# Splitting a table tile in two, holding back later transfers, and a third matmul in place of a vector sum in the first 14 of 256 steps

## The chip, the cores and the metric

One core of a Trainium2 chip runs the whole kernel. The metric is the device time of one execution in microseconds (us), and smaller is better. Each kernel was executed several times, with runs of the kernel before on the same chip beside it. All times compared below are of the fast state. One run of the kernel before (1415.36 us) was disturbed; it stands in the quoted range and medians of the first rounds, not in any ratio.

## The reference, cut to what matters

```python
# x: 8 x 3136 x 256, w_in: 256 x 1024, conv_w: 3 x 1024, w_out: 1024 x 256, float32 and float64
X = np.fft.fft(x, axis=1)
X = np.fft.fft(X, axis=2).real.astype(np.float32)
h = np.maximum(X @ w_in, 0.0)
conv_out = sum(conv_w[k] * shifted(h, k - 1) for k in range(3))   # along the sequence, zeros at the ends
gate = 1.0 / (1.0 + np.exp(-conv_out))
out = (h * gate @ w_out).astype(np.float32)
```

The kernel writes the transform along the sequence as products with tables of cosines and sines. For each batch it makes two arrays, `PT` and `QT`, over half of the sequence positions. With the transform along the features folded into the first weight matrix (`G`), `A` comes from `PT` and `B` from `QT`. The hidden row is relu(A + B) on the front half of the sequence and relu(A - B), mirrored, on the back half.

## The kernel before

The tables lie in one tile with six slots. Slots 0 and 1 serve the even frequencies, 2 and 3 the odd ones, and 4 and 5 are copies of 3 and 2 with changed signs.

```python
    tab = const.tile([P, 6, HQ, HE], F32, name="tab")
    ...
    def load_tables(par):
        st = slice(2 * par, 2 * par + 2)
        to = tab[:, st].rearrange("p s q i -> p s (q i)")
        for i in range(2):
            nc.sync.dma_start(out=to[i:NP:2], in_=dft_seq[0:NP // 2, st, HQ * i:HQ * (i + 1)] ...)

    def mend_tables(par, half):                      # runs on ScalarE
        st = slice(2 * par, 2 * par + 2)
        row = tab[96:NP, st, HQ - 1]
        act(row, row, AF.Copy, scale=half[96:NP])                              # L216
        if par:
            for i in range(2):
                for to, of, s in ((4, 3, -1.0), (5, 2, 1.0)):
                    act(tab[0:KR, to, :, i:HO:2], tab[0:KR, of, :, i:HO:2], AF.Copy,   # L220
                        scale=-s if i else s)
    ...
    for par in (1, 0):
        mend_tables(par, half)
    ...
    for i, u in enumerate(us[j] for j in (0, 1, 4, 2, 3, 5, 6, 7, 8)):   # the transform of batch 0
        u.matmuls(0, 1)
        u.copy()                                     # ScalarE
        if i == 2:
            flip()
        u.fin()                                      # VectorE
        if i < 2:
            w_in[0].narrow(i, slice(0, H))           # VectorE: float64 weights to float32
        ...
```

`us` lists the units of the transform: 0 and 1 use the odd tables, 4 (the last feature, with matmuls of one column, `ea`) and 2, 3 the even ones, 5 and 6 the odd ones again, 7 and 8 the even ones.

Then 256 steps follow, each for one batch, one of four chunks of the sequence and one of eight blocks of 128 hidden features. Before a step's products, ScalarE writes the last feature's part of A into `pa` (the "seed", L499), from a row `er` that was broadcast by DMA and a column `ge` of the folded weights. `pa` and `pb`, which PE writes, lie in PSUM; the other tiles lie in SBUF:

```python
    def products(s):                                 # PE
        mm(pb[s][:, 0:n], G[0:P - 1, 1, fs], PQ[b][1][0:P - 1, ch.k0:ch.k1], True, True)     # B
        mm(pa[s][:, 0:n], G[:, 0, fs], PQ[b][0][:, ch.k0:ch.k1], False, True)                # A, onto a seed
    def copies(s):                                   # ScalarE: +B and -B into SBUF
        for i, cols in enumerate((ch.fcols, ch.cols)):
            act(nb[s][:, i, cols], p[:, cols], AF.Copy, scale=-1.0 if i else 1.0)            # L514
    def combine(s):                                  # VectorE: two sums with relu
        for i, (to, cols) in enumerate(((h[:, ch.front], ch.fcols), (h[:, ch.back][:, ::-1], ch.cols))):
            nc.vector._custom_dve(TENSOR_ADD_SAT, out=to, in0=a[:, cols], in1=c[:, i, cols], s0=BIG, s1=0.0)  # L525
    ...
    def gate(s):
        v, p, r = shares(s)                          # two halves of the row
        gt(g[:, p], g[:, p], h[:, p], op=ALU.mult)   # GpSimd, L557
        vt(g[:, v], g[:, v], h[:, v], op=ALU.mult)   # VectorE, L558
```

Between `combine` and `gate` lie a first tap on ScalarE, two taps on VectorE and the sigmoid on ScalarE. After `gate` the second product runs on PE (`mm2`). In the first steps VectorE narrows the rest of the weights too (L402 to L409) and folds the input of batch 1 (L151 to L179). In program order `gate` of a step is followed on VectorE by `combine` of a later step and then by that side work.

## Time and profile before

| kernel before | |
|---|---|
| time, median of 3 runs | 1278.77 us (1276.97 to 1415.36) |
| PE begins the transform | 46.08 us |
| first sum of the main loop (L525) | 70.98 us |
| step 14's gate product on VectorE (L558) starts | 173.19 us |

In the views PE is TensorE's matmuls and PEld its weight loads, DVE is VectorE, ACT ScalarE, POOL GpSimd; L525 is line 525 of the kernel's file. The granted clock is the share of full speed that TensorE had. First, two lines of the start: ScalarE's copy of unit 0, which follows PE's start at 46.08, and the one-column products of the even unit 4 (start us, us, what, and in brackets the idle time before and what ended it):

```profile
48.44 0.32 ACT L282 COPY as<-po 128x196 f32<-128x196 f32 x1 [1.45 <-PE po L90]
...
52.96 0.89 PE L90 MATMUL po<-tab,ea 99*1 99x197 f32 x16
```

### The profile page before, as it was taken

To read this page: it belongs to the slowest core of one execution; us is meant where nothing else is said; L and a number is where in the kernel's file an instruction comes from. 1 tells how busy PE (TensorE), PEld (TensorE's weight loads), DVE (VectorE), ACT (ScalarE), POOL (GpSimd) and SP (SyncE) were. 2 spreads that over 40 slices of the span, in tenths; PEclk is the share of its full clock that TensorE was granted. 3 is DMA by queue.
4 is the path that set the end of the run, shared out by engine and by line. 5 is a ranking of instruction groups with operands and counts; after the bars stand their busy time and mean duration, and the time that the engine had idled before them with its cause. 6 is when DMAs were issued, how large, how long until landed. Compare 5 with 4: busy or idle time off the path is not lost.

```text
span 1277.4 us, 15522 instructions
## 1 busy us (share of the span) xinstructions
PE 1178.4 (92%) x4850; PEld 887.1 (69%) x4850; DVE 1148.4 (90%) x1753; ACT 885.1 (69%) x1835; POOL 397.6 (31%) x500
## 2 busy tenths in 40 slices
PE   0567799999999999999999999999999999999997
PEld 0345567767777777777677776777777777777776
DVE  4579998999999989899989989999999878899996
ACT  0244676777767777777777777776777778788884
POOL 3311643424342315242423414242222212222222
PEclk9988999999999999999999999999999999999999
DMA  8420321202031103020111202120010001011000
GB/s 212 121 63 1 119 69 31 83 28 76 27 94 32 56 25 95 25 83 25 39 57 51 61 25 88 32 67 16 25 44 32 30 26 38 23 32 34 26 25 30
DMA packets 47179, 66.07 MB, mean 52 GB/s; under 512 B 5684, under 2 KB 35276, under 8 KB 47096
## 3 DMA queue, kind: packets, MB, share of 16 engines
q1 hardware_dynamic: 41668, 51.93, 13.5%
q0 software_dynamic: 5120, 12.85, 3.6%
q8 instruction: 39, 0.64, 0.2%
q14 instruction: 44, 0.36, 0.1%
q10 hardware_dynamic: 308, 0.29, 0.1%
HBM read 39.26 MB, written 25.74 MB: 51 GB/s over the span
## 4 chain that ended last, share of the span: by engine, by line
PE 64%; DVE 21%; issue 5%; DMA 4%; ACT 4%; POOL 1%; SPq 0%; DVEq 0%; ACTq 0%; POOLq 0%
PE po L90 40%; PE pb L90 9%; PE pa L90 9%; PE pd L90 6%; DVE g L537 6%; DVE h L525 4%; DMA tab<-dft_seq_dram 3%; DVE g L558 3%; ACT nb L514 2%; DVE xh L151 1%; DVE xh L162 1%; DVE w L178 1%; ACT g L550 1%; DVE w L179 1%; DVE xh L167 0%
## 5 line engine op out<-in xcount | busy, mean ns | idle before, releaser
L90 PE MATMUL po<-wout,g 128*128 128x256 f32 x3072 | 716.3, 383 | 37.5 <-DVE g L558 34.0
L90 PEld LDWEIGHTS po<-wout,g 128*128 128x128 f32 x3072 | 579.7, 191 | 200.7 <-DVE g L558 78.4
L537 DVE SCALAR_TENSOR_TENSOR g<-h,cw,g 128x770 f32<-128x770 f32 (+1 forms) x512 | 555.2, 1084 | 10.6 <-ACT g L531 1.5
L557 POOL TENSOR_TENSOR g<-g,h 128x385 f32<-128x385 f32 (+1 forms) x256 | 240.7, 941 | 762.6 <-ACT g L550 544.2
L550 ACT ACTIVATE g<-g 128x385 f32<-128x385 f32 (+2 forms) x512 | 244.4, 528 | 223.2 <-DVE g L537 223.0
L514 ACT ACTIVATE nb<-pb 128x386 f32<-128x386 f32 (+3 forms) x512 | 225.6, 494 | 83.5 <-PE pb L90 82.6
L525 DVE CUSTOM_DVE_ANT_0 h<-pa,nb 128x386 f32<-128x386 f32 (+3 forms) x512 | 264.8, 558 | 0.9 <-PE pa L90 0.9
L531 ACT ACTIVATE g<-h,cw 128x770 f32<-128x770 f32 (+1 forms) x256 | 243.6, 951 | 0.2 <-DVE h L525 0.2
L90 PE MATMUL pb<-qt,G 127*128 127x387 f32 (+2 forms) x512 | 214.3, 499 | 2.6 <-ACT nb L514 2.4
L90 PE MATMUL pa<-pt,G 128*128 128x387 f32 (+2 forms) x512 | 212.6, 496 | 0.4 <-DVE pt L267 0.4
L499 ACT ACTIVATE pa<-eb,ge 128x387 f32<-128x387 f32 (+2 forms) x256 | 154.0, 602 | 3.1 <-DVE h L525 3.1
L558 DVE TENSOR_TENSOR g<-g,h 128x385 f32<-128x385 f32 (+1 forms) x256 | 151.3, 591 | 1.2 <-ACT g L550 1.2
L90 PEld LDWEIGHTS pa<-pt,G 128*128 128x128 f32 x512 | 96.9, 189 | 74.3 <-issue 18.9
L90 PE MATMUL pd<-tab,w 99*128 99x196 f32 (+2 forms) x448 | 117.4, 374 | 0.0
L90 PEld LDWEIGHTS pb<-qt,G 127*128 127x128 f32 x512 | 93.9, 190 | 25.8 <-ACT nb L514 4.7
L126 POOL DMA_INDIRECT xh<-in_x_dram,idx x64 | 95.9, 1498 | 18.1 <-issue 12.3
L90 PEld LDWEIGHTS pd<-tab,w 99*128 99x128 f32 (+1 forms) x448 | 82.9, 190 | 12.8
L577 ACT COPY os<-po 128x256 f32<-128x256 f32 x196 | 58.1, 397 | 10.6 <-PE po L90 6.2
L151 DVE TENSOR_TENSOR xh<-xh 98x1020 f32<-98x1020 f32 (+1 forms) x32 | 44.4, 1391 | 12.6 <-DMA xh<-in_x_dram,idx 10.3
L90 PE MATMUL po<-tab,w 98*128 98x196 f32 (+4 forms) x64 | 18.0, 442 | 38.3 <-POOL w L182 25.9
L90 PEld LDWEIGHTS po<-tab,w 98*128 98x128 f32 (+1 forms) x64 | 13.3, 224 | 42.0 <-POOL w L182 26.0
L162 DVE TENSOR_TENSOR xh<-xh 98x1024 f32<-98x1024 f32 (+1 forms) x32 | 40.1, 1252 | 0.1
(93 smaller groups left out, 365.2 us busy)
## 6 DMA issues: line engine op xcount, KB each, us to landing
out_dram<-os SPq DMA_DIRECT2D x192, 128.0 KB
xh<-in_x_dram SPq DMA_DIRECT2D x16, 784.0 KB
eb<-ed SPq DMA_DIRECT2D x16, 193.5 KB
tab<-dft_seq_dram SPq DMA_DIRECT2D x4, 601.8 KB
raw<-in_moe_w_in_dram SPq DMA_DIRECT2D x2, 1024.0 KB
raw<-in_moe_w_out_dram SPq DMA_DIRECT2D x1, 2048.0 KB
eb<-ed SPq DMA_DIRECT2D x8, 209.0 KB
eb<-ed SPq DMA_DIRECT2D x8, 193.0 KB
```

The costliest lines, as they stand in the source:

```text
L90: nc.tensor.matmul(o, l, r, start=start, stop=stop, skip_group_check=True)
L126: nc.gpsimd.indirect_dma_start(out=xh[b, h][0:NP, 7 - m].rearrange("p q d -> p (q d)"), out_offset=None, in_=bass.AP(tensor=x.tensor, offs ...
L151: vt(a[:, :, :, 1:D], a[:, :, :, 1:D], r[:, :, :, D - 1:0:-1], op=ALU.add)
L499: act(pa[s][:, 0:n], eb[b, c], AF.Copy, scale=ge[:, f:f + 1])
L514: act(nb[s][:, i, cols], p[:, cols], AF.Copy, scale=-1.0 if i else 1.0)
L525: nc.vector._custom_dve(TENSOR_ADD_SAT, out=to, in0=a[:, cols], in1=c[:, i, cols], s0=BIG, s1=0.0)
L531: act(gs[s], hs[s][:, 0:n], AF.Copy, scale=cw[:, 0, s[2]:s[2] + 1])
L537: stt(out=g, in0=h[:, k:k + n], scalar=cw[:, k, f:f + 1], in1=g, op0=ALU.mult, op1=ALU.add)
L550: act(gs[s][:, c], gs[s][:, c], AF.Sigmoid)
L557: gt(g[:, p], g[:, p], h[:, p], op=ALU.mult)
L558: vt(g[:, v], g[:, v], h[:, v], op=ALU.mult)
L577: nc.scalar.copy(out=osb[:, j % 2], in_=pt[:, j % 2])
```

## The change

There are three intents. Each parity of tables gets a tile of its own, so that work on the odd tables need not wait for the even ones. Memsets on tiles that are about to be loaded ("holds") make later transfers wait for GpSimd's gathers of the input (in the trace after, the odd tables are issued at 9.82 us, behind a memset at 9.62; before, at 1.68); the small row of the input's second half is also issued ahead of the tables. And in the first 14 steps, where VectorE is full (busy 85.77 of 88.70 us from 71.0 to 159.7 us before), PE adds B onto A with a third product, so that ScalarE can write relu(A + B) straight from PSUM; this takes one of the two sums from VectorE. The back half still needs a sum, (A + B) - 2B.

```diff
+TRIPLE = 14
+    def hold(t):
+        nc.gpsimd.memset(t[0:1, 0, 0, 0:1], 0.0)
...
-    tab = const.tile([P, 6, HQ, HE], F32, name="tab")
+    tabs = [const.tile([P, n, HQ, HE], F32, name="tab%d" % n) for n in (2, 4)]
...
-    for f in ops[0:1] + ops[2:]:
-        f()
+    plain, zero, *mirrored = load_ops(0, 1, nc.sync, held=True)
+    plain()
+    zero()
+    for f in mirrored[0:2]:
+        f()
+    hold(tabs[1])
+    for f in mirrored[2:4]:
+        f()
     load_tables(1)
-    load_row0()
-    ops[1]()
     for i in range(2):
+        if w_in[i].raw is not None and i == 0:
+            hold(w_in[i].raw)
         w_in[i].load(nc.sync)
...
+    def triple(s):
+        return s[0] == 0 and s[1] * NF + s[2] < TRIPLE
...
-        mm(pa[s][:, 0:n], G[:, 0, fs], PQ[b][0][:, ch.k0:ch.k1], False, True)
+        mm(pa[s][:, 0:n], G[:, 0, fs], PQ[b][0][:, ch.k0:ch.k1], False, not triple(s))
+        if triple(s):
+            mm(pa[s][:, 0:n], G[0:P - 1, 1, fs], PQ[b][1][0:P - 1, ch.k0:ch.k1], False, True)
...
+        if triple(s):
+            act(nb[s][:, 1, ch.cols], p[:, ch.cols], AF.Copy, scale=-2.0)
+            row_of(s)
+            act(hs[s][:, ch.front], pa[s][:, ch.fcols], AF.Relu)
+        else:
+            for i, cols in enumerate((ch.fcols, ch.cols)):
+                act(nb[s][:, i, cols], p[:, cols], AF.Copy, scale=-1.0 if i else 1.0)
...
+            if i or not triple(s):
+                nc.vector._custom_dve(TENSOR_ADD_SAT, out=to, in0=a[:, cols], in1=c[:, i, cols],
+                                      s0=BIG, s1=0.0)
```

Line numbers shift: L216 and L220 become L223 and L227; the sums L525 become L556; GpSimd's and VectorE's gate products L557 and L558 become L588 and L589; the narrowing L402 and L403 become L409 and L410; the fold L151 becomes L158; PE's helper L90 becomes L91.

More of the change, by code (lines that the diff above doesn't have):

```diff
@@ L105, with load_ops @@
     nc.gpsimd.memset(sg[:, 1], 1.0)
-    def load_ops(b, h, eng):
+    def hold(t):
+        nc.gpsimd.memset(t[0:1, 0, 0, 0:1], 0.0)
+    def load_ops(b, h, eng, held=False):
         def plain():
@@ L112, in plain @@
             xh[b, h] = t
+            if held:
+                hold(t)
             eng.dma_start(out=t[0:NP, 0:4], in_=bass.AP(
@@ L190, in fold_ops, with table @@
         return half(0) + half(1)
-    tab = const.tile([P, 6, HQ, HE], F32, name="tab")
+    tabs = [const.tile([P, n, HQ, HE], F32, name="tab%d" % n) for n in (2, 4)]
     PQ, eb, er = {}, {}, {}
     ed = edp.tile([B, NK], F32, name="ed")
+    def table(k, st, q, cols):
+        return tabs[st // 2][0:k, st, q, cols] if st < 2 else tabs[1][0:k, st - 2, q, cols]
     def load_tables(par):
         st = slice(2 * par, 2 * par + 2)
-        to = tab[:, st].rearrange("p s q i -> p s (q i)")
+        to = tabs[par][:, 0:2].rearrange("p s q i -> p s (q i)")
         for i in range(2):
@@ L203, in load_tables @@
                               .rearrange("p s q i -> p s (q i)"))
-    def load_row0():
         n = HQ * HE
-        nc.sync.dma_start(out=tab[NP:KR, 0:4].rearrange("p s q i -> p s (q i)"), in_=bass.AP(
-            tensor=dft_seq.tensor, offset=dft_seq.offset + (NP * 4 * NQ - HQ + 2) * HE,
-            ap=[[n, 1], [NQ * HE, 4], [1, n]]))
+        nc.sync.dma_start(out=to[NP:KR], in_=bass.AP(
+            tensor=dft_seq.tensor, offset=dft_seq.offset + ((NP * 4 + 2 * par) * NQ - HQ + 2) * HE,
+            ap=[[n, 1], [NQ * HE, 2], [1, n]]))
     def mend_tables(par, half):
-        st = slice(2 * par, 2 * par + 2)
-        row = tab[96:NP, st, HQ - 1]
+        row = tabs[par][96:NP, 0:2, HQ - 1]
         act(row, row, AF.Copy, scale=half[96:NP])
@@ L218, in mend_tables @@
             for i in range(2):
-                for to, of, s in ((4, 3, -1.0), (5, 2, 1.0)):
-                    act(tab[0:KR, to, :, i:HO:2], tab[0:KR, of, :, i:HO:2], AF.Copy,
+                for to, of, s in ((2, 1, -1.0), (3, 0, 1.0)):
+                    act(tabs[1][0:KR, to, :, i:HO:2], tabs[1][0:KR, of, :, i:HO:2], AF.Copy,
                         scale=-s if i else s)
@@ L244, in f @@
             k = KR if q == HQ - 1 else NP
-            mm(p[o], w(k, q), tab[0:k, st, q, cols], start, stop)
+            mm(p[o], w(k, q), table(k, st, q, cols), start, stop)
         return f
@@ L447 @@
     nc.scalar.dma_start(out=dm, in_=dft_dim[:, :, 0:2])
-    for f in load_ops(0, 0, nc.sync):
-        f()
-    ops = load_ops(0, 1, nc.sync)
-    for f in ops[0:1] + ops[2:]:
+    ops = load_ops(0, 0, nc.sync)
+    for f in ops:
+        f()
+    plain, zero, *mirrored = load_ops(0, 1, nc.sync, held=True)
[5 more added lines that the diff above has]
+    for f in mirrored[2:4]:
         f()
     load_tables(1)
-    load_row0()
-    ops[1]()
     for i in range(2):
+        if w_in[i].raw is not None and i == 0:
+            hold(w_in[i].raw)
         w_in[i].load(nc.sync)
@@ L499, in seed, with row_of @@
         act(pa[s][:, 0:n], eb[b, c], AF.Copy, scale=ge[:, f:f + 1])
+    def triple(s):
+        return s[0] == 0 and s[1] * NF + s[2] < TRIPLE
+    def row_of(s):
+        hs[s] = hp.tile([P, HW], F32, name="h", tag="h")
+        w = chunks[s[1]].w
+        if chunks[s[1]].zeros:
+            nc.gpsimd.memset(hs[s][:, 0:w:w - 1], 0.0)
     def products(s):
@@ L512, in copies @@
         nb[s] = nbp.tile([P, 2, HN], F32, name="nb", tag="nb")
-        for i, cols in enumerate((ch.fcols, ch.cols)):
-            act(nb[s][:, i, cols], p[:, cols], AF.Copy, scale=-1.0 if i else 1.0)
+        if triple(s):
[5 more added lines that the diff above has]
+                act(nb[s][:, i, cols], p[:, cols], AF.Copy, scale=-1.0 if i else 1.0)
     def combine(s):
@@ L519, in combine @@
         a, c = pa.pop(s), nb.pop(s)
-        h = hp.tile([P, HW], F32, name="h", tag="h")
-        hs[s] = h
-        if ch.zeros:
-            nc.gpsimd.memset(h[:, 0:ch.w:ch.w - 1], 0.0)
+        if not triple(s):
+            row_of(s)
+        h = hs[s]
         for i, (to, cols) in enumerate(((h[:, ch.front], ch.fcols), (h[:, ch.back][:, ::-1], ch.cols))):
-            nc.vector._custom_dve(TENSOR_ADD_SAT, out=to, in0=a[:, cols], in1=c[:, i, cols],
-                                  s0=BIG, s1=0.0)
+            if i or not triple(s):
+                nc.vector._custom_dve(TENSOR_ADD_SAT, out=to, in0=a[:, cols], in1=c[:, i, cols],
+                                      s0=BIG, s1=0.0)
     def first_tap(s):
```

## The prediction

> **What bounds the kernel now.** I read the page first (busy shares, the 40 slices), then busy time by stretch, then the chain in order of time, then the waits of the first 70 us.
>
> ```profile
> span 1277.4 us, 15522 instructions
> PE 1178.4 (92%) x4850; PEld 887.1 (69%) x4850; DVE 1148.4 (90%) x1753; ACT 885.1 (69%) x1835; POOL 397.6 (31%) x500
> PE   0567799999999999999999999999999999999997
> DVE  4579998999999989899989989999999878899996
> DMA  8420321202031103020111202120010001011000
> ```
>
> TensorE is full from the seventh slice on; the 99 us that it lacks (1277.4 less 1178.4) lie mostly in the first six slices of 32 us, where VectorE or the transfers are full instead. By stretch:
>
> ```profile
> 0.00:33.00 33.00, 0.91 (x3) 0.85 (x4) 16.05 (x25) 2.41 (x3) 13.02 (x26) 1.00 0.83 213
> 33.00:46.00 13.00, 0.67 (x2) 0.15 (x1) 3.19 (x5) 3.21 (x4) 2.71 (x3) 1.00 0.85 204
> 46.00:69.00 23.00, 22.92 (x104) 16.79 (x104) 13.24 (x28) 6.12 (x16) 7.30 (x11) 1.00 0.31 96
> 106.40:113.60 7.20, 5.84 (x16) 4.13 (x16) 6.96 (x14) 3.04 (x8) 0.91 (x2) 0.76 0.00 1
> 145.00:149.65 4.65, 4.16 (x16) 2.96 (x16) 4.61 (x9) 3.04 (x8) 0.93 (x2) 1.00 0.46 142
> ```
>
> Columns after the length: busy us of PE, PE's weight loads, DVE, ACT, POOL, then granted clock, share of the DMA engines, GB/s. There are three stages: to 46 us almost no matmul runs, the DMA engines are 83 to 85% busy; from 46 to 69 us PE is full with the first transform; from 69 to about 165 us (the last two rows are one step each, of the 256 of the main loop) DVE is busy 97 to 99% while PE has room. After that PE leads. A microsecond taken from any of the first three stages should arrive at the end whole, as nothing later waits for the clock on the wall.
>
> The chain and the waits of the start:
>
> ```profile
> 1.68 17.59 DMA tab<-dft_seq_dram
> 20.65 21.98 DMA tab<-dft_seq_dram
> 42.79 3.24 ACT tab L220 x4
> 46.08 14.73 PE po L90 x62
> ```
> ```profile
> ACT tab L220 <- DMA tab<-dft_seq_dram: 15.7, 1, 15.7
> PE po L90 <- ACT tab L220: 12.4, 1, 12.4
> ```
>
> The four L220 copies make tables 4 and 5 from 2 and 3 (odd frequencies). These landed by 26.2 us, where the mend at L216 ran (0.94 us). Yet L220 waited to 42.79: the last transfer of tables 0 and 1 landed just then (20.65 + 21.98 = 42.63). The copies don't read tables 0 and 1, so this wait is false, made by the single tile.
>
> [...] from 16 to 20 us, with mostly tables moving, the DMA share is 0.46 [...] at 173 GB/s[...]; from 28 to 42 us, all engines busy, it is 223 GB/s, 14 each. [...] the second half of x folds only from 27.45 us, after a small row of it, issued by 14.1 us, came in behind the tables. [...] In the trace the copies of `nb` take 482 ns; whether relu equals that no run shows yet. [...]
>
> **The change, part by part.**
>
> *Own tiles.* They remove the false wait of 15.7 us. But what stood behind it does not all go: after the two odd units (14 matmuls, 6.95 us from 46.08) the next unit needs tables 0 and 1 themselves. So the start becomes the later of two chains.
>
> *Order of transfers.* [...] the second x half goes after GpSimd's fourth gather (6.08 + 0.97, so 7.1 us), the tables after the sixth (about 9.9), the weights after the eighth (about 12.4)[...]. Odd tables: [...] about 28.8 us. [...] even tables at 39.6, mended (0.95 us) at 40.6.
>
> *Two chains.* Odd: 28.8 + 0.94 + 3.24 + 6.95 = 39.9 us. Even: 40.6 us, rounded with hand-overs to 41. Before, PE came there at 52.96. **Gain 12 us.** x itself arrives much earlier (its fold now ends at 36.3; I expect the odd weights `w` near 24.5 in place of 32.5), but is no longer what comes last, so this gains nothing more.
>
> *Three products in 14 steps.* Before, a step has two ScalarE copies of B and two VectorE sums (L525: 551 ns each, 1.02 us the pair, so the second adds 0.47). After, one sum goes, one copy becomes a relu of the same 386 columns [...], and PE adds one product: a pair of passes, 0.65 us from start to start (pb at 142.67, pa at 143.33). In the first ten steps DVE has weight narrowing of some 2.3 us besides (steps of 5 to 7.3 us, PE at most 5.8 busy of 7.2, at a low clock): 10 x 0.47 = 4.7 us gained. In the last four DVE's step is 4.65 and PE's work is 2.69 + 1.31 = 4.00; with 0.65 it is 4.65, so PE takes DVE's place: gain 0. **Gain 4.7 us.** PE's 14 x 0.65 = 9.1 us are hidden in its gaps.
>
> Sum: 12 + 4.7 = 16.7; 1278.8 - 16.7 = 1262.1.
>
> **The rivals.** (a) The even tables become the bound and land as late as before, 42.6 us[...]. PE then starts them at 43.7: gain 9.2, 1265. (b) Full relief: the odd tables at 26, the even ones at 36, and each of 14 steps 0.47 us shorter: 15 + 6.6 gives 1257. Against: 4.65 of PE in the last steps. (c) A new wait: the row that the feature unit takes (issued at 54.36 before, to land in 1.9 us on a free queue) is now issued at about 41 us[...]; ScalarE's sign flip behind it holds up its copies. [...] Against: its users are the seeds, first at 69.1 us, some 5 us after the broadcasts had come[...]. If it bites, 3 to 5 us go: 1266. (d) The third product delays ScalarE's relu and with it the seeds. Against: products end about 2 us before `nb` is copied (103.72 + 0.81 against 106.79). Worth under 2 us.
>
> **Range and chances.** The start gives 8 to 16 us, the steps 2 to 7, with little correlation: 10 to 23. Run scatter of the fast state is 2 us (1276.97 and 1278.77; 1415 was a disturbed run). Predicted 1262, range 1254 to 1270. Faster by over 2% needs under 1253.2, a gain of 25.6, beyond even rival (b): 7%. Slower needs a loss that nothing here suggests: 2%. Within 2%: 91%.
>
> **What would show it.** Right: L220 follows L216 at once, at about 30 us; PE begins `tab` work at 30 to 34 and the `ea` products near 41 in place of 52.96; the first L525 near 59 in place of 70.98; L525 14 fewer; steps 0 to 9 shorter by some 0.5 us, steps 10 to 13 not, with PE idle under 0.2 us in them. Wrong: PE starting the even units before 37 or after 44; steps 10 to 13 getting faster too; ScalarE waiting over 4 us for the `er` row with PE idle behind it; a reload of the activation tables within the steps.

The landing times in it, 28.8 us for the odd tables and 39.6 us for the even ones, and the loss of 3 to 5 us in rival (c) are estimates of mine that no trace of the kernel before shows.

## More of the kernel before

Third, the timeline of one such step (start us, us, what):

```profile
100.24 1.02 DVE L525 CUSTOM_DVE_ANT_0 h<-pa,nb 128x385 f32<-128x385 f32 x2
...
100.49 0.87 POOL L557 TENSOR_TENSOR g<-g,h 128x385 f32<-128x385 f32 x1 [5.14 <-ACT g L550]
...
101.17 0.37 DVE L402 TENSOR_SCALAR wout<-raw 128x256 int32<-128x256 int32 x1
```

GpSimd's gate product runs from 100.49 to 101.36. It lies almost whole beside the pair of sums (100.24 to 101.26), each of which reads one operand from PSUM (`pa`) and one from SBUF (`nb`).

Second, VectorE's groups from the first sum to step 14. The columns are: line, engine and operation, names and shapes, count; busy us, mean ns of one; idle us before it.

```profile
L525 DVE CUSTOM_DVE_ANT_0 h<-pa,nb 128x386 f32<-128x386 f32 x19 | 9.7, 551 | 0.0
L558 DVE TENSOR_TENSOR g<-g,h 128x385 f32<-128x385 f32 x15 | 8.3, 553 | 0.0
...
L151 DVE TENSOR_TENSOR xh<-xh 99x1020 f32<-99x1020 f32 x2 | 3.3, 1648 | 0.0
L402 DVE TENSOR_SCALAR wout<-raw 128x256 int32<-128x256 int32 x8 | 2.9, 359 | 0.0
...
L403 DVE TENSOR_SCALAR wout<-wout 128x256 int32<-128x256 int32 x8 | 2.4, 294 | 0.3
```

## The result, and the profile after

The changed kernel takes 1268.22 us (median of 4 runs, 1267.65 to 1271.40), against 1277.96 us for the kernel before in the same rounds. The ratio is 0.9931, with a 95% interval of 0.9909 to 0.9954: within 2%. Ratios in this document are the mean time of one kernel's fast runs over that of the other's of the same rounds, so they are not quite the ratios of the medians that are quoted. The result is correct.

So the class and the range (1254 to 1270) held. The gain is 9.7 us by the medians (8.8 by the means of the fast runs), where 16.7 was forecast. The page after:

```profile
span 1265.7 us, 15557 instructions
PE 1186.2 (94%) x4878; PEld 891.4 (70%) x4878; DVE 1146.4 (91%) x1739; ACT 885.4 (70%) x1835; POOL 397.9 (31%) x503
PE   0877999899999999999999999999999999999998
DVE  6499998999999989899899989998999878899996
```

PE has 28 instructions more (14 products of two passes) and VectorE 14 fewer, yet VectorE's busy time fell by only 2.0 us (1148.4 to 1146.4), where 14 sums of 0.47 us would be 6.6. PE is 8 tenths full in the second slice, where it was 5.

Two stages by stretch, as in the prediction but with borders where they now end (to the first mend of a table, and from PE's start on the transform to the seeds):

```profile
0.00:29.30 29.30, 0.59 (x2) 0.49 (x2) 17.45 (x27) 1.46 (x2) 14.47 (x29) 1.00 0.93 227
...
33.65:59.30 25.65, 23.57 (x104) 16.62 (x104) 13.23 (x28) 6.24 (x15) 7.35 (x12) 1.00 0.37 127
```

The stretch with an idle PE and busy transfers ends at 33.65 in place of 46 us. But the first transform, which filled PE before (22.92 of 23.00 us), now takes 25.65 us and leaves PE idle for 2.08. The timeline of the start shows where (the bracket gives the idle time before and what ended it):

```profile
29.34 0.94 ACT L223 ACTIVATE tab<-tab,half 2x786 f32<-2x786 f32 x1 [22.39 <-DMA tab<-dft_seq_dram]
30.32 3.28 ACT L227 ACTIVATE tab<-tab 99x784 f32<-99x784 f32 x4
...
33.65 6.86 PE L91 MATMUL po<-tab,w 99*128 99x196 f32 x14 [2.27 <-ACT tab L227]
...
40.32 0.94 ACT L223 ACTIVATE tab<-tab,half 2x786 f32<-2x786 f32 x1 [6.72 <-DMA tab<-dft_seq_dram]
...
41.28 0.32 ACT L289 COPY as<-po 128x196 f32<-128x196 f32 x1
41.36 0.89 PE L91 MATMUL po<-tab,ea 99*1 99x197 f32 x16 [0.85 <-ACT tab L223]
...
47.24 2.90 PE L91 MATMUL po<-tab,w 98*128 98x392 f32 x8 [0.67 <-DVE qt L307]
...
62.24 0.56 DVE L556 CUSTOM_DVE_ANT_0 h<-pa,nb 128x385 f32<-128x385 f32 x1 [1.95 <-ACT h L542]
```

The false wait is gone: L227 follows L223 at once, at 30.32. PE's odd units start at 33.65, 12.4 us earlier than before, and the even ones (`ea`) at 41.36, 11.6 us earlier. L289 is ScalarE's copy of unit 0, which before followed PE's start by 2.36 us (48.44 after 46.08). Now it is executed at 41.28, 7.6 us after PE's start, after the mend of the even tables, which stands ahead of it in ScalarE's program and waits 6.72 us for a transfer. The chain that ended last passes exactly there:

```profile
16.32 23.92 DMA tab<-dft_seq_dram
...
40.32 0.94 ACT tab L223
...
41.28 0.33 ACT as L289
...
42.27 0.35 DVE win L409
```

Not PE but ScalarE's copy and VectorE's narrowing carry the chain from the even tables on. Of the 11.6 us that PE gained at the `ea` products, 8.74 are left at the first sum (62.24 against 70.98).

These are differences of single traces. The profiled run of the kernel before took 1279.17 us, 1.5 more than the mean of its fast runs, and in triple_only below, which has the same start, the `ea` products come at 52.09 in place of 52.96. So a time of the start is known to about 1 us. The length of steps 1 to 14 repeats better: 79.22 to 79.63 us in the five traces with one sum a step and GpSimd's half left as it is.

And the steps did not get shorter. VectorE's groups from the first sum to step 14, as shown of the kernel before:

```profile
L589 DVE TENSOR_TENSOR g<-g,h 128x385 f32<-128x385 f32 x15 | 9.0, 598 | 0.0
L556 DVE CUSTOM_DVE_ANT_0 h<-pa,nb 128x386 f32<-128x386 f32 x13 | 6.9, 552 | 0.0
...
L409 DVE TENSOR_SCALAR wout<-raw 128x256 int32<-128x256 int32 x8 | 4.5, 560 | 0.0
...
L158 DVE TENSOR_TENSOR xh<-xh 99x1020 f32<-99x1020 f32 x2 | 4.2, 2115 | 0.0
...
L410 DVE TENSOR_SCALAR wout<-wout 128x256 int32<-128x256 int32 x8 | 3.7, 463 | 0.3
```

The sums still take 552 ns. But untouched instructions got longer: L409 takes 560 ns where L402 took 359, L410 takes 463 where L403 took 294, the fold L158 on 99 partitions 2115 where it took 1648, the gate product L589 598 where it took 553. The step that answers to the one above:

```profile
96.49 0.55 DVE L556 CUSTOM_DVE_ANT_0 h<-pa,nb 128x385 f32<-128x385 f32 x1
...
96.75 0.87 POOL L588 TENSOR_TENSOR g<-g,h 128x385 f32<-128x385 f32 x1
96.96 0.81 DVE L409 TENSOR_SCALAR wout<-raw 128x256 int32<-128x256 int32 x1
```

With one sum gone, L409 comes while GpSimd's product (96.75 to 97.62) still runs, and it ends at 97.77, 0.15 us after that. It takes 0.81 us for work that elsewhere takes 0.28.

I read two stretches from each trace: from the first sum to the start of the first gate product (the ramp: three steps without a GpSimd product), and from there to the gate product of step 14.

| us | kernel before | after | difference |
|---|---|---|---|
| `ea` products start | 52.96 | 41.36 | -11.60 |
| from these to the first sum | 18.02 | 20.88 | +2.86 |
| ramp | 22.69 | 21.45 | -1.24 |
| steps 1 to 14 | 79.52 | 79.34 | -0.18 |
| gate product of step 14 | 173.19 | 163.03 | -10.16 |

### The profile page after: what moved, and what is told of

It is laid out like the page before. It is cut to its first block, busy times and chain, and to the rows that moved or that the text cites. A ratio compares the mean times of both kernels' runs of the same rounds, so it can differ in the third digit from the quotient of the medians.

```text
span 1265.7 us, 15557 instructions
## 1 busy us (share of the span) xinstructions
PE 1186.2 (94%) x4878; PEld 891.4 (70%) x4878; DVE 1146.4 (91%) x1739; ACT 885.4 (70%) x1835; POOL 397.9 (31%) x503
## 4 chain that ended last, share of the span: by engine, by line
PE 62%; DVE 23%; issue 5%; DMA 4%; ACT 4%; POOL 1%; SPq 0%; DVEq 0%; ACTq 0%; POOLq 0%
PE po L91 38%; PE pb L91 9%; PE pa L91 8%; DVE g L568 7%; PE pd L91 6%; DVE h L556 3%; DVE g L589 3%; DMA tab<-dft_seq_dram 2%; ACT nb L545 2%; DVE xh L158 1%; DVE xh L169 1%; DVE w L185 1%; ACT g L581 1%; DMA er<-qt 1%; DVE w L186 1%
## 5 line engine op out<-in xcount | busy, mean ns | idle before, releaser
L91 PE MATMUL po<-wout,g 128*128 128x256 f32 x3072 | 715.4, 382 | 32.4 <-DVE g L589 28.7
L91 PEld LDWEIGHTS po<-wout,g 128*128 128x128 f32 x3072 | 579.0, 190 | 194.5 <-DVE g L589 71.5
L588 POOL TENSOR_TENSOR g<-g,h 128x385 f32<-128x385 f32 (+1 forms) x256 | 239.2, 935 | 743.5 <-ACT g L581 528.7
L545 ACT ACTIVATE nb<-pb 128x386 f32<-128x386 f32 (+2 forms) x484 | 213.6, 494 | 83.0 <-PE pb L91 81.6
L556 DVE CUSTOM_DVE_ANT_0 h<-pa,nb 128x386 f32<-128x386 f32 (+2 forms) x498 | 258.2, 558 | 1.9 <-ACT h L542 1.9
L91 PE MATMUL pb<-qt,G 127*128 127x387 f32 (+2 forms) x512 | 213.9, 498 | 0.8 <-ACT nb L540 0.8
L91 PE MATMUL pa<-pt,G 128*128 128x387 f32 (+2 forms) x512 | 212.1, 495 | 0.9 <-ACT pa L513 0.5
L589 DVE TENSOR_TENSOR g<-g,h 128x385 f32<-128x385 f32 (+1 forms) x256 | 152.0, 594 | 1.2 <-ACT g L581 1.2
L91 PEld LDWEIGHTS pa<-pt,G 128*128 128x128 f32 x512 | 96.6, 189 | 75.4 <-issue 18.7
L91 PE MATMUL pd<-tab,w 99*128 99x196 f32 (+2 forms) x448 | 117.4, 374 | 0.0
L91 PEld LDWEIGHTS pb<-qt,G 127*128 127x128 f32 x512 | 94.0, 190 | 23.4 <-issue 3.5
L133 POOL DMA_INDIRECT xh<-in_x_dram,idx x64 | 98.1, 1533 | 17.9 <-issue 12.4
L91 PEld LDWEIGHTS pd<-tab,w 99*128 99x128 f32 (+1 forms) x448 | 82.9, 190 | 12.8
L158 DVE TENSOR_TENSOR xh<-xh 98x1020 f32<-98x1020 f32 (+1 forms) x32 | 45.5, 1421 | 7.4 <-DMA xh<-in_x_dram,idx 7.4
L91 PE MATMUL po<-tab,w 98*128 98x196 f32 (+4 forms) x64 | 18.2, 442 | 26.6 <-ACT tab L223 23.7
L169 DVE TENSOR_TENSOR xh<-xh 98x1024 f32<-98x1024 f32 (+1 forms) x32 | 40.5, 1266 | 0.1
L91 PEld LDWEIGHTS po<-tab,w 98*128 98x128 f32 (+1 forms) x64 | 13.1, 222 | 30.6 <-issue 26.0
```

What stands on the lines that cost most here:

```text
L91: nc.tensor.matmul(o, l, r, start=start, stop=stop, skip_group_check=True)
L133: nc.gpsimd.indirect_dma_start(out=xh[b, h][0:NP, 7 - m].rearrange("p q d -> p (q d)"), out_offset=None, in_=bass.AP(tensor=x.tensor, offs ...
L158: vt(a[:, :, :, 1:D], a[:, :, :, 1:D], r[:, :, :, D - 1:0:-1], op=ALU.add)
```

## The experiments

Two things were to be explained: where 2.86 us of the start went, and why the sums that were removed gave almost nothing. For the steps my theory was that GpSimd's product, formerly beside the sums that read PSUM, now holds up the next VectorE instruction. It rests on the trace above: L409 takes 0.81 us beside that product, for work that elsewhere takes 0.28, while the sum beside it keeps its 0.55 us. The sums read one input from PSUM; the fold and the narrowing read SBUF alone. Whether this is what tells them apart no run tests. I had not looked at it in the prediction. The rival was the prediction's own: PE, with a third product, becomes the bound. For the start my theory was the order of ScalarE's program (called C in the expectations), with the feature row of the prediction's rival (c) against it.

All kernels, with the start of the first sum and the length of steps 1 to 14 from the trace. Each has four to six runs in all, and the kernels under one heading share a job and its runs of the kernel before.

| kernel | median us (range) | ratio (95% interval) | first sum | steps 1 to 14 |
|---|---|---|---|---|
| start_only | 1270.05 (1268.90 to 1270.52) | 0.9942 (0.9928 to 0.9955) | 62.65 | 80.44 |
| triple_only | 1275.73 (1275.49 to 1279.28) | 0.9999 (0.9985 to 1.0013) | 71.21 | 79.63 |
| no_pool_mult, wrong | 1261.56 (1260.68 to 1264.28) | 0.9881 (0.9866 to 0.9896) | 64.20 | 71.88 |
| start_no_pool_mult, wrong | 1268.10 (1265.00 to 1270.77) | 0.9935 (0.9920 to 0.9950) | 60.94 | 76.97 |
| **second job** | | | | |
| late_mend | 1271.15 (1266.15 to 1273.85) | 0.9944 (0.9926 to 0.9963) | 61.62 | 79.22 |
| small_share | 1266.76 (1265.90 to 1271.23) | 0.9908 (0.9893 to 0.9922) | 68.85 | 76.74 |
| tiles_no_hold | 1271.61 (1267.94 to 1274.27) | 0.9944 (0.9927 to 0.9960) | 63.76 | 80.44 |
| both_mends | 1264.66 (1263.96 to 1268.37) | 0.9898 (0.9886 to 0.9911) | 64.44 | 76.84 |
| **third job** | | | | |
| after_again | 1268.02 (1267.18 to 1272.54) | 0.9931 (0.9915 to 0.9947) | 61.59 | 79.34 |
| odd_first | 1265.53 (1265.23 to 1265.78) | 0.9899 (0.9885 to 0.9914) | 59.44 | 79.60 |
| odd_first_small | 1262.69 (1262.15 to 1263.16) | 0.9878 (0.9863 to 0.9892) | 59.34 | 76.79 |
| **fourth job** | | | | |
| odd_first_small_no_hold | 1262.77 (1261.95 to 1263.64) | 0.9877 (0.9860 to 0.9893) | 60.75 | 76.79 |

The medians of the kernel before in the four jobs are 1277.20, 1278.47, 1278.06 and 1278.40 us. All kernels but the two marked ones are correct.

### The two halves of the change

start_only keeps the tiles and holds, with two sums in every step:

```diff
-TRIPLE = 14
+TRIPLE = 0
```

> The changed start (own tiles, holds) with the steps as before. Theory A (the third product's relief in the steps is given back, so nearly all of the gain is the start's): first sum on VectorE near 61.2 us, 9.8 before the old 70.98; that lead stays constant through the steps (gate product of step 14 near 163.4 against 173.19 before and 163.03 in the change); time near 1268.5, 0.99 to 0.995 of before. Theory B (my prediction: the steps give 4.7 us and the start is what fell short): lead of 5 us, time near 1273.

triple_only is the kernel before with the third product, the relu and the single sum of the diff above, and nothing else of it.

> The three products in 14 steps with the old start. Theory A: the gate product of step 14 within 1 us of the old 173.19; time within 0.1% of before; the VectorE instruction right after the single sum is 0.5 to 0.7 us longer than its kind, and ends when GpSimd's product ends. Theory B: 4.7 us earlier, 1273.3.

The third product alone is worth nothing: ratio 0.9999, within 0.15% either way. Steps 1 to 14 take 79.63 us against 79.52 before, the ramp 21.04 against 22.69, and the first sum comes at 71.21 against 70.98. The start alone carries the gain. In start_only's trace the lead over the kernel before is 8.33 us at the first sum and 7.40 at step 14, not the constant 9.8 that I expected. That start_only lies some 2 us above the whole change in the medians is not resolved; the intervals of the ratios overlap, and the start scatters in a way that comes below.

### GpSimd's product away

In no_pool_mult and start_no_pool_mult the first 14 steps leave out GpSimd's half of the gate product. The result is wrong (relative error 0.162 in both).

```diff
-        gt(g[:, p], g[:, p], h[:, p], op=ALU.mult)
+        if not (b == 0 and c * NF + f < 14):
+            gt(g[:, p], g[:, p], h[:, p], op=ALU.mult)
```

> The change without GpSimd's product in the first 14 steps (wrong result on purpose: half of the gate product is missing there). Theory A (GpSimd's 0.87 us product holds up VectorE's next instruction now that only one sum runs beside it): the first weight-narrowing instruction back at 0.29 us, steps 2 to 9 shorter by 0.5 to 0.6 us, the last four bound by PE at 4.65 to 4.8; gate product of step 14 at 157 to 158.5 against 163.03; time near 1263. Rival (PE's third product or ScalarE's relu is what sets the step): step lengths unchanged, 1268.

> The start alone, without GpSimd's product in the same 14 steps (wrong result on purpose). Theory A: two sums of 1.02 us cover GpSimd's product, so taking it away saves under 1.5 us in all: gate product of step 14 at 162 to 163.4. Rival (GpSimd's product costs VectorE the same whatever runs beside it): 5 us saved, as in the run with the third product.

Together with start_only and the change this makes a square of four. Steps 1 to 14 in us:

| | two sums | one sum, third product | the third product saves |
|---|---|---|---|
| GpSimd multiplies its half | 80.44 | 79.34 | 1.10 |
| it does not | 76.97 | 71.88 | 5.09 |

Steps 1 to 14 hold the single sums of eleven triple steps (a sum runs two steps ahead of its gate product), and 11 x 0.47 is 5.2 us. So the removed sums give nearly their full 0.47 us each once GpSimd's product is out of the way, and little while it is there. VectorE's groups in no_pool_mult agree:

```profile
L158 DVE TENSOR_TENSOR xh<-xh 99x1020 f32<-99x1020 f32 x2 | 2.4, 1210 | 0.0
...
L410 DVE TENSOR_SCALAR wout<-wout 128x256 int32<-128x256 int32 x8 | 2.4, 294 | 0.3
L409 DVE TENSOR_SCALAR wout<-raw 128x256 int32<-128x256 int32 x8 | 2.3, 284 | 0.0
```

560, 463 and 2115 ns are back to 284, 294 and 1210. My expectation for two sums without GpSimd's product was missed: I thought that it would save under 1.5 us, and it saves 3.47 (80.44 to 76.97). In the kernel before, too, GpSimd's product costs VectorE something (L402 at 359 and L151 at 1648 ns show it): the pair of sums covers it only in part.

The rival fell as well. no_pool_mult shows what PE needs in a triple step, as it is full there:

```profile
127.69 0.81 PE L91 MATMUL pb<-qt,G 127*128 127x387 f32 x2
...
132.24 0.81 PE L91 MATMUL pb<-qt,G 127*128 127x387 f32 x2
...
136.79 0.82 PE L91 MATMUL pb<-qt,G 127*128 127x387 f32 x2
```

The first product of one step comes 4.55 us after that of the step before. The prediction said 4.65, so its estimate of PE was good. But VectorE went on at 4.06 to 4.12 us a step meanwhile (between the starts of the gate products at 122.69, 126.76, 130.88, 135.00 and 139.06): PE fell behind by under 0.5 us a step, and VectorE did not wait for it in these few steps (busy 9.03 of 9.10 us from 127.69 to 136.79). In the change itself VectorE takes 4.62 us (138.94 to 143.56), and PE is full there too (4.62 of 4.62 us): the two are level, but it is VectorE that gets faster when GpSimd's product goes. How long PE could lag so, with more such steps, no run shows.

### A smaller share for GpSimd

If GpSimd's product is the trouble, a quarter of the row in place of a half should shorten what it holds up, at the price of a longer product on VectorE.

```diff
-        return slice(0, n // 2), slice(n // 2, n), slice(n, w)
+        m = n * 3 // 4 if triple(s) else n // 2
+        return slice(0, m), slice(m, n), slice(n, w)
```

> The change with GpSimd's share of the gate product cut from a half to a quarter in the 14 steps; VectorE takes the rest. Theory A: GpSimd's product falls from 0.87 to about 0.45 us and ends with or before the single sum, so the next VectorE instruction is not held up (0.6 saved), for 0.2 us more of VectorE's own product: 0.3 to 0.4 us a step, gate product of step 14 near 158.5; time 4 to 5 us less than the change. Rival (step set by PE or ScalarE): step 0.2 us longer or unchanged.

Steps 1 to 14 fall from 79.34 to 76.74 us, 2.6 in place of the 4 to 5 expected. The step shown above now reads:

```profile
102.58 0.53 POOL L589 TENSOR_TENSOR g<-g,h 128x193 f32<-128x193 f32 x1
...
102.79 0.47 DVE L409 TENSOR_SCALAR wout<-raw 128x256 int32<-128x256 int32 x1
```

GpSimd takes 0.53 us in place of 0.87 and ends at 103.11; L409 ends at 103.26, again 0.15 us later. The stretch is down to 0.19 us, not to nothing, and VectorE's own part of the gate grew from 0.55 to 0.75 us.

### Where the start lost its 2.86 us

late_mend moves the mend of the even tables behind the copies of units 0 and 1 in ScalarE's program:

```diff
-    for par in (1, 0):
-        mend_tables(par, half)
+    mend_tables(1, half)
...
     for i, u in enumerate(us[j] for j in (0, 1, 4, 2, 3, 5, 6, 7, 8)):
+        if i == 2:
+            mend_tables(0, half)
         u.matmuls(0, 1)
```

> The change with ScalarE's mend of the even tables put behind the copies of the first two units instead of ahead of them. Theory C (the mend, which waits for the even tables until 40.3 us, holds the copy of the first odd unit behind it in ScalarE's order, and with it VectorE's weight narrowing, which PE's weight products then wait for): copy of the first unit near 36.1 in place of 41.28, first narrowing done near 40, no PE wait for the narrowed weights, first sum on VectorE near 60.3 in place of 62.24; time 1.5 to 2 us less than the change. Rival (the row of the feature unit, [...] is what holds ScalarE and PE): the row still lands at 49, first sum unchanged at 62.2.

Its timeline:

```profile
35.84 0.32 ACT L289 COPY as<-po 128x196 f32<-128x196 f32 x1 [2.42 <-PE po L91]
...
41.27 0.88 PE L91 MATMUL po<-tab,ea 99*1 99x197 f32 x16 [1.43 <-ACT tab L223]
...
48.08 0.92 ACT L349 ACTIVATE er<-er 1x392 f32<-1x392 f32 x1 [4.56 <-DMA er<-qt]
...
54.26 0.16 ACT L492 COPY ge<-po 128x4 f32<-128x4 f32 x1 [1.09 <-PE po L91]
```

The copy of unit 0 is at 35.84, not 41.28. From the `ea` products to ScalarE's copy of the weight column (L492) it takes 12.99 us, where the change takes 14.76 (41.36 to 56.12) and the kernel before took 13.00 (52.96 to 65.96). So 1.76 us of the loss is the order of ScalarE's program, and late_mend gets all of it back. The feature row is still waited for, until 48.08, without a loss: rival (c) of the prediction happened as a wait (5.6 us in the change) and cost nothing. The other 1.09 us is the third product in the first step, where nothing covers it: from the seeds to the first sum it takes 2.94 us (59.30 to 62.24), and took 1.85 (69.13 to 70.98). triple_only and late_mend have the same 2.94 or 2.95. 1.76 + 1.09 = 2.85.

Yet late_mend is no faster in time (1271.15 us, with 7.7 us between its fastest and slowest run). This was a miss of my expectation, and the granted clock shows one reason. Over its six runs the mean clock was 0.995 and 0.994 at 1266.15 and 1266.86 us, and 0.989 to 0.991 at 1273.38 to 1273.85. The trace is of the run of 1266.86 us. Columns as in the prediction:

```profile
50.00:54.00 4.00, 4.00 (x22) 2.57 (x20) 2.47 (x7) 1.17 (x2) 3.21 (x4) 1.00 0.29 92
54.00:58.00 4.00, 4.00 (x18) 4.00 (x19) 0.87 (x2) 0.49 (x2) 1.26 (x6) 0.70 0.64 200
```

From 54 to 58 us PE's granted clock is 0.70, and from 58 to 62 us 0.88, just before the first sum (61.62). By an estimate from these two means this is 0.50 (the clock of small_share from 46 to 50 us) for 3.4 us, from 55.6 us on. In small_share it struck earlier and longer:

```profile
42.00:46.00 4.00, 1.00 (x16) 0.42 (x16) 0.72 (x3) 1.27 (x2) 0.00 (x0) 0.60 0.45 162
46.00:50.00 4.00, 4.00 (x19) 3.58 (x12) 3.72 (x8) 1.26 (x4) 0.00 (x0) 0.50 0.27 103
50.00:54.00 4.00, 4.00 (x16) 3.95 (x15) 3.83 (x8) 1.12 (x2) 1.03 (x2) 0.62 0.02 9
```

There the even tables landed late as well (L223 ran at 43.96 us; where it waited for the transfer it ran between 39.67, in after_again, and 43.96), and from the `ea` products to the first sum it took 23.85 us in place of the change's 20.88. The new wait of PE for the even tables thus does two things: it passes the scatter of their landing on to the end, and a lowered clock comes with a long wait. Nine traces have this wait just before the `ea` products. In the four where it was 0.85 to 1.72 us (after, after_again, late_mend, start_no_pool_mult) the clock was 1.00 from 42 to 50 us; in the five where it was 1.73 to 4.64 us (no_pool_mult, tiles_no_hold, both_mends, start_only, small_share) it fell to a mean of 0.50 to 0.73 in at least one of the two slices of 4 us. So the first sums in the table are not to be compared without the clock. With 1.72 and 1.73 on either side, the length of the wait alone need not be what decides, and late_mend's fall, at 55.6 by the estimate above, comes 14 us after its wait, with PE busy 20.27 of the 20.35 us from the `ea` products to the first sum.

### Tiles without holds, and both remedies at once

tiles_no_hold is start_only with a `hold` that returns at once. both_mends joins late_mend and small_share.

> Own tiles and the new order of issue without the holds, steps as before. Theory: the false wait is gone, but the even tables still land near 42 us instead of 40.2[...]: feature products near 43.5 against 41.4; time 1 to 2 us over the start with holds. Rival (the holds bring the gain): feature products after 46 and time near before.

> Late mend and small share together: the two losses are in different stages, so they add: first sum near 60.3, gate product of step 14 near 156.7, time 6 to 7 us less than the change, about 1261.5, and 1.3% faster than before. Rival (they overlap): no more than the larger of the two.

Without holds: 0.9944, with them (start_only): 0.9942. The holds are worth nothing that these runs can see. I had expected the `ea` products at 43.5 us without them; they came at 41.50. both_mends is faster than the change (1264.66 us, 0.9898), by its shorter steps (76.84 us). That the two gains add was not borne out: I had expected a first sum near 60.3 and 1261.5 us. In its trace the even tables came late, PE waited 2.85 us, the clock was 0.50 from 42 to 46 us, and the first sum came at 64.44.

### The odd units first

The better remedy for the start is to give PE something else while the even tables travel. Units 5 and 6 need only the odd tables.

```diff
-    for par in (1, 0):
-        mend_tables(par, half)
+    mend_tables(1, half)
-    for i, u in enumerate(us[j] for j in (0, 1, 4, 2, 3, 5, 6, 7, 8)):
+    for i, u in enumerate(us[j] for j in (0, 1, 5, 6, 4, 2, 3, 7, 8)):
+        if i == 4:
+            mend_tables(0, half)
...
-        if i == 2:      # flip; further down the store and the broadcasts
+        if i == 4:
```

odd_first_small adds the quarter share for GpSimd, odd_first_small_no_hold also takes the holds away. after_again is the change itself once more, for the same rounds.

> The change once more, on the same chip as the two below. If the start's loss hangs on whether PE's wait for the even tables falls so that the clock is halved, its first sum lies between 62.2 (no halving before 60 us) and 67 us; median near 1268 to 1270.

> The change with all four units that need only the odd tables ahead of those that need the even ones, and ScalarE's mend of the even tables behind their copies. Theory D (between the even tables' coming, 41.3, and the first sum, the change loses 1.76 us to PE waits behind ScalarE's order and, by luck, up to 4 us to a halved clock after PE's wait for the tables): PE has work from 33.6 us on without a wait, granted clock 1.00 to 60 us, the copy of the weight column near 53.6 to 54.5 in place of 56.1, first sum at 59 to 60; gate product of step 14 at 160 to 161; time 2 to 3 us less than the change in the same rounds. Rival (the feature row is needed earlier than it now comes: broadcasts land after 57 us): ScalarE's seeds wait for a DMA, first sum at 62 or later, no gain.

> The same with GpSimd's share a quarter in the 14 steps. Theories A and D: steps 1 to 14 take 76.7 us as in the run with the small share alone (79.3 in the change), so 2.6 us less than the run above: gate product of step 14 near 158, time near 1263, 0.988 of before: the best of all correct versions.

> The best version without the holds. In it PE never waits once it has begun, so what the holds are worth shows without luck of the clock. Theory (the holds bring x 5 us earlier, but the odd tables come last and come no later without them): PE's third product 0.7 us earlier (32.9 against 33.7), all else equal; time within 1 us of the best version, 1262 to 1263. Rival (the holds are a real part of the gain): PE's third product 2 us later or more, time 1264.5 to 1266.

The chain of odd_first that ended last, and two stretches of it:

```profile
30.42 3.28 ACT tab L227 x4
...
33.74 14.45 PE po L91 x62
```

```profile
42.00:46.00 4.00, 4.00 (x29) 2.25 (x28) 3.79 (x9) 1.73 (x5) 0.00 (x0) 1.00 0.46 174
46.00:50.00 4.00, 4.00 (x18) 2.96 (x17) 1.77 (x5) 2.12 (x6) 1.49 (x3) 1.00 0.17 64
```

PE works from 33.74 us without waiting for a table, at a clock of 1.00, the first sum comes at 59.44, and the runs lie within 0.6 us where those of the change lie within 5.4 (after_again). In the same rounds it is 2.5 us faster than the change by the medians, and the quarter share takes off another 2.8. odd_first_small, at 1262.69 us (0.9878), beats both the kernel before and the change, and the same without holds is as fast (1262.77 us, 0.9877).

The clock can fall in this order too. In the trace without holds PE waited once, for 1.03 us before 46.74, and from 54 to 58 us its clock was 0.63, though it is counted busy for all of these 4.00 us:

```profile
54.00:58.00 4.00, 4.00 (x16) 3.68 (x15) 0.92 (x3) 0.74 (x3) 1.62 (x6) 0.63 0.62 183
```

Its first sum came at 60.75 us in place of 59.34. My expectation, that PE never waits in this version, was missed, though its time was met.

## Why the prediction was right or wrong, point by point

**The start, right.** The false wait, its removal and the two chains came out as said: the odd mend at 29.34 us (said 28.8), the even mend done at 41.26 (40.6), PE at the `ea` products at 41.36 (41). The gain there is 11.6 us, and 12 was said. That the earlier input gains nothing holds too.

**The carrying over, wrong by 2.9 us.** "A microsecond taken from any of the first three stages should arrive at the end whole" is the step that failed. Of 11.6 us, 8.74 reached the first sum. The prediction had put the mend of the even tables into PE's chain only. It did not ask what else stands behind that instruction on ScalarE: the copy of unit 0, and behind it VectorE's narrowing (1.76 us, regained in late_mend). The rest is the third product in the first step, which rival (d) had named with under 2 us and the sum had left out (1.09 us). From the first sum on, gains did arrive whole: 8.74 there, and 10.16 at step 14 with what the steps gave.

**The steps, wrong in their reason.** "10 x 0.47 = 4.7 us gained" failed. The sums went, those left kept their duration, and the relu costs nearly what the copies do (median 484 ns beside 474, and 482 before; with two table loads in the whole run before and after). But steps 1 to 14 shortened by 0.18 us and the ramp by 1.24. (The narrowing, put at some 2.3 us a step, is 2.5 in the same trace; it enters no sum.) Less the 1.09 that the third product costs in the first step, the part is worth 0.3 us by the traces, and triple_only at 0.9999 says the same. What took the sum's place is GpSimd's product: it now falls on instructions that take longer beside it (L409 560 ns, L410 463 and L158 2115, against 284, 294 and 1210 without it in no_pool_mult). The groups other than the sum that I showed (21.4 us in place of 16.9), with two more of the fold (L169 and L185, each on 98 partitions, 4.8 in place of 3.9), take 26.2 us, and took 20.8: 5.4 us of stretching against 14 x 0.47 = 6.6 us of sums. That remainder of 1.2 us agrees with the 1.42 us of the ramp and the steps together.

**PE in the last steps, right in size and wrong in effect.** The estimate of 4.65 us a step is 4.55 measured. It was to take VectorE's place with idle time "under 0.2 us" in four steps. In the change PE was busy 18.37 of 19.40 us there (129.50 to 148.90), so it was nearly full. But PE did not set the steps: without GpSimd's product VectorE passed the triple steps at 4.06 to 4.12 us beside the same work of PE.

**The rivals.** (a) did not happen in the change, but the scatter of the landing brings it about in single runs: in small_share PE came to the even units at 45.00 us, where (a) said 43.7. (b) did not happen. (c) happened as a wait without a cost. (d) cost 1.1 us.

**The range.** It held with 1.8 us to spare at its upper end: a start of 8.7 and steps of 1.4 make 10.2 us in the traces, and 9.7 by the medians. The start alone was enough for it. The steps' part lay below its own range of 2 to 7 us, and the start near the lower end of its 8 to 16: that the sum still held owes something to luck.

## What to carry to other kernels

Before counting a removed VectorE instruction as time saved, look at what GpSimd does beside it: here GpSimd's product cost 3.5 us over steps 1 to 14 beside two sums and 7.5 beside one. The sums, which read PSUM, took 551 to 552 ns with it; the narrowing that moved up into the place of one took 0.81 us in place of 0.28 in the step shown, and ended 0.15 us after that product. When a false wait is removed, follow every engine's program order behind the instruction that now waits, not only the chain that you meant to shorten. And fill a real wait with work that needs other data: the order of the units gave more, and steadier, than moving the mend alone or holding transfers back.
